# Turning the first batch's sums between the second batch's products, with other engines for the copies and another order of mixing

## The chip, the cores and the metric

The kernel runs on one core of a Trainium2 chip. Its engines have a queue of instructions each and work at the same time: TensorE (PE in the profile, its weight loads PEld), VectorE (DVE), ScalarE (ACT), GpSimd (POOL) and SyncE (SP), which issues the DMAs. An engine takes its instructions in order; an instruction that waits holds up all behind it on that engine. The metric is the time on the device in microseconds (us), as a median of several runs.

## The reference

Attention with a local window and block summaries, and behind it a mixing layer with low rank and a layer of 2048 hidden values, in fp32. There are 4 batches, 8 heads, 768 tokens, 64 values a head, so a row of 512 values for each token.

```python
scores_l = scale * q @ k^T          # kept where |i - j| < 16
scores_s = scale * q @ max over blocks of 32 of k + log(32)
a = softmax([scores_l, scores_s])
x = a @ [v, means over blocks of 32 of v]     # (batch, 768, 512)
h = x^T @ U @ V                               # mixing over tokens, rank 32
u = x + h^T
out = u + relu(u @ w_ch1) @ w_ch2             # 512 -> 2048 -> 512
```

## The kernel before

The order of all instructions is written by hand: the schedule is manual, so each engine's queue has the order of the program's text. Products in full precision are made of fp32r parts: a value is split into a high part (a copy by ACT) and the rest (a subtraction by DVE or POOL), and three products of parts are added (`split`).

PSUM has 8 banks of 128x512 fp32. Tiles of `bank` get them in the order in which they came free in the program, and a bank is free when the last instruction that reads it is done. Copies, temporary rows and outputs share 8 places in SBUF, the tag `val`, by the same rule.

*The first batch* (`sts[0]`) goes through the hidden layer while its weights arrive, are converted, split and stored for later (the loop over `f`, 16 tiles of 128 hidden values). For each `f` and each half `hf` of the tokens (384), `up` makes the hidden values (12 matmuls into a bank) and `down_rows` adds the product with the second weight to sums (9 matmuls). The sums are `accs[0]` and `accs[1]`: three banks each, 128 tokens by 512 values, held through the whole loop; two banks are left for all else. In between, one step of the second batch's attention and mixing has its place after each product (`place`, 58 steps at places 6 to 63; the last seven are `operand_steps(st, 1)`).

`operand_steps` first adds mixing's product to the rows `st.x`, two tiles of 128 tokens at a time (`mix_rows` with k = 0, 1, 2: two matmuls L730, an addition on DVE L734), then turns tokens to columns (`turn_tokens`, L739, with k = 0, 1 for token tiles 3 to 5 and k = 2, 3 for tiles 0 to 2) and makes and splits the operands of the next batch's products (`operands`).

*The hand-over.* When the first batch's sums are done, each sum is copied out of PSUM (`leave_rows`, L955), turned by three PE transposes per 128 columns (`finish_rows`, L963), added to `u`'s two parts on DVE (L966 reads PSUM and SBUF, L967 reads two SBUF tiles) and sent out by a DMA on SP's queue (L968). A half has four such finishes, c = 0 to 3. In the kernel before, the first half's copies stand before the last nine matmuls L942 of the second half, its four finishes right behind them; then come the second half's copies, and its four finishes stand in the list `behind`.

*The other batches* use a scheme with fewer products for the up layer (`up_phase`): per pair p of hidden tiles seven products of six matmuls (L1203) into banks x and y, with results moved by ACT (L1225, L1237, L1249, L1262) and DVE (L1229, L1242, L1263). `up_phase` yields after each product; the loop at the end of the program counts these steps from i = 0 and puts the next batch's attention and the list `behind` between them. Pair 0 has five steps (its last two products come in pair 1's turn), each later one seven: x, y, third and second of the pair before among them. After four of a pair's products `prepare` splits the next unit of stored weights (ACT L186, POOL L187); when both units of a loaded piece are split, a DMA for the next piece (`whole<-up`, L877) is issued four steps later. These DMAs, the outputs L968 and the next batch's loads (k L208, q L214 and L215, v rows L253) stand in one SP queue. The next batch's steps stand at i = 4, 7, 10, 14, 17, 20 and so on: scores at 4 and 14 (24 small matmuls, L377), exponentials at 4, 7, 14 and 17 (DVE L403, ACT L413), key maxima (L319, L336) at 7, a transpose on DVE (L433) and five loads at 10.

The entries of `behind` are spread by

```python
ends = spread(behind, 2, 2 + 2 * len(behind))   # every second step from i = 2
...
do(steps.get(i, ()))    # the next batch's attention
do(ends.get(i, ()))     # the entries of behind
tick()                  # weight loads that are due
```

Of the kernel before, what the change touches and what calls it, by code (L numbers as in the profile page):

```python
# [32 lines left out]
NC = DM // P  # L33
# [48 lines left out]
def f32(ap):  # L82
    return ap.bitcast(F32)
# [3 lines left out]
def body(ctx: ExitStack, tc, q0, q1, k, v, vn, uv, w1, w2, mask, ident, rep, out):  # L87
    nc = tc.nc
# [10 lines left out]
    def bank(name):  # L99
        return psum.tile([P, 512], F32, name=name, tag="bank")  # L100
# [13 lines left out]
    def op_place(k):  # L114
        return wt.tile([P, 4 * NH], F32, name="place", tag=f"op{k}")
# [18 lines left out]
    for i in range(4):  # L134
        t = op_place(i)
# [57 lines left out]
    def new_batch(b):  # L193
        st = Batch()
        st.b = b
        st.qt, st.kt, st.km, st.vt, st.vn, st.vsum, st.neg = ({} for _ in range(7))
        st.e, st.at, st.psx, st.t4, st.u = ({} for _ in range(5))
        st.op, st.tmp, st.h = ({} for _ in range(3))
        st.ps_s, st.ps_t, st.ps_m, st.ps_r, st.ps_u, st.ps_n = ({} for _ in range(6))
        return st  # L200
# [392 lines left out]
        mix_s_out(st, c, 2)  # L593

    def operand_steps(st, i):
        return [(mix_rows, st, i, k) for k in range(3)] + [(operands, st, i, k) for k in range(4)]

    def one_bank_steps(st):

# [48 lines left out]
        for n, x in enumerate(operand_steps(st, 0)):  # L648
            todo.insert(at + 2 + 2 * n if n < 6 else todo.index((products, H - 1)), x)
        return todo + [(mix, st, 2), (mix_back, st, 2)] + operand_steps(st, 1)  # L650

    def later_steps(st):

        todo = [(later_step, st, i) for i in range(STEPS)]
        for n, x in enumerate(operand_steps(st, 0)):
            todo.insert(MIX[0] + 3 + 2 * n, x)
        return todo + operand_steps(st, 1)
# [278 lines left out]
    def down_rows(acc, f, g, first, last):  # L936

        gh, gl = g
        for t in range(NH // P):
            sl = slice(t * P, (t + 1) * P)  # L940
            for j, (part_w, gt) in enumerate(((0, gh), (0, gl), (1, gh))):
                nc.tensor.matmul(  # L942
                    acc[t],
                    gt[:, sl],
                    w_split[1, f][:, part_w],
                    start=(first and j == 0),
                    stop=(last and j == 2),
                )

    def leave_rows(acc):  # L950

        rows = []
        for t, ps in enumerate(acc):
            r = mo.tile([P, DM], F32, name="r", tag="val", bufs=VALS)
            (nc.vector.tensor_copy if t == 1 else nc.scalar.copy)(r, ps)  # L955
            rows.append(r)
        return rows

    def finish_rows(st, hf, rows, c):

        ps = bank("ps_o")
        for t, r in enumerate(rows):
            nc.tensor.transpose(ps[:, t * P : (t + 1) * P], r[:, c * P : (c + 1) * P], ident_sb)  # L963
        o = mo.tile([P, DM], F32, name="o", tag="val", bufs=VALS)[:, :NH]
        uh, ul = st.u[hf]
        nc.vector.tensor_tensor(o, ps[:, :NH], f32(uh)[:, c], ALU.add)  # L966
        nc.vector.tensor_tensor(o, o, f32(ul)[:, c], ALU.add)  # L967
        nc.sync.dma_start(out=out[c, :, hf * NH : (hf + 1) * NH], in_=o)  # L968


    sts = [new_batch(b) for b in range(B)]
# [3 lines left out]
    st = sts[0]  # L975
# [183 lines left out]
    accs = [None, None]  # L1159
    prev = None  # L1160
    for f in range(NF):
# [27 lines left out]
        run(turn)  # L1189
        turn = begin_turn(f + 3)  # L1190
    rows = leave_rows(accs[0])
    down_rows(accs[1], NF - 1, prev[2], False, True)
    for c in range(NC):
        finish_rows(st, 0, rows, c)
    rows = leave_rows(accs[1])


    def product(ps, a, b, first=False):
# [115 lines left out]

    UP, DOWN = 7 * NF // 2 - 2, NF * NU
    FIRST_STEPS = 15
    behind = [(finish_rows, sts[0], 1, rows, c) for c in range(NC)]
    for b in range(1, B):
        cur, ahead, after = ([*sts, None, None][b + i] for i in range(3))
        todo = later_steps(ahead) if ahead else []  # L1320
# [25 lines left out]
        behind = [(finish, cur, hf, c) for hf in range(2) for c in range(NC)]  # L1346
# [94 lines left out]
```

## Time and profile before

| | |
|---|---|
| median of 3 runs | 666.86 us (666.3 to 669.9) |
| the profiled execution | 668.33 us |
| its span, first to last instruction | 666.50 us |
| granted TensorE clock, mean | 0.997 |
| PE, busy | 640.6 us (96% of the span) |
| DVE, busy | 371.7 us (56%) |
| ACT, busy | 358.5 us (54%) |
| POOL, busy | 361.0 us (54%) |
| DMA | 116.13 MB, mean 174 GB/s |

The span is the profiled execution's from its first instruction to its last; the time has 1.83 us around it. Busy shares are means over the whole span, and stages differ. Rows of the timeline give the start from the span's beginning, the length, the engine, the line, the operation, what is written and read, and in brackets the idle time before and what ended it. A modelled matmul is longer than its distance to the next, since matmuls overlap. The hand-over from the first batch to the second lies at about 223 us.

### The profile page before, as it was taken

To read this page: it belongs to the slowest core of one execution; us is meant where nothing else is said; L and a number is where in the kernel's file an instruction comes from. 1 tells how busy PE (TensorE), PEld (TensorE's weight loads), DVE (VectorE), ACT (ScalarE), POOL (GpSimd) and SP (SyncE) were. 2 spreads that over 40 slices of the span, in tenths; PEclk is the share of its full clock that TensorE was granted. 3 is DMA by queue.
4 is the path that set the end of the run, shared out by engine and by line. 5 is a ranking of instruction groups with operands and counts; after the bars stand their busy time and mean duration, and the time that the engine had idled before them with its cause. 6 is when DMAs were issued, how large, how long until landed. Compare 5 with 4: busy or idle time off the path is not lost.

```text
span 666.5 us, 14015 instructions
## 1 busy us (share of the span) xinstructions
PE 640.6 (96%) x5232; PEld 562.6 (84%) x5232; DVE 371.7 (56%) x1006; ACT 358.5 (54%) x803; POOL 361.0 (54%) x402
## 2 busy tenths in 40 slices
PE   5899999999999898999999999999999999999997
PEld 4789889988888797997787899997787899998885
DVE  5578866668777763567544645566644521232223
ACT  4666666655553555765453467665453365553322
POOL 5424975965577676762336487662334375653310
PEclk9999999999999998999999999999999999999999
DMA  8997497766774268787457059787441055331002
GB/s 219 228 367 239 135 315 240 230 173 195 227 225 163 72 178 265 213 251 203 147 142 205 25 171 325 228 247 204 138 143 59 24 171 178 112 126 64 32 1 94
DMA packets 76420, 116.13 MB, mean 174 GB/s; under 512 B 6976, under 2 KB 52928, under 8 KB 76352
## 3 DMA queue, kind: packets, MB, share of 16 engines
q1 hardware_dynamic: 76352, 115.24, 57.1%
q8 instruction: 41, 0.67, 0.4%
q14 instruction: 27, 0.22, 0.1%
HBM read 91.10 MB, written 24.12 MB: 173 GB/s over the span
## 4 chain that ended last, share of the span: by engine, by line
PE 83%; DVE 4%; DMA 4%; ACT 3%; POOL 2%; issue 2%; SPq 1%; ACTq 0%; POOLq 0%; DVEq 0%
PE acc L1288 30%; PE ps_h L1203 25%; PE acc L942 7%; PE ps_h L920 7%; PE ps_x L494 3%; PE ps_s L354 2%; PE ps_o L739 2%; PE ps_s L377 2%; DMA place<-in_uv 1%; DMA place<-in_q 1%; PE ps_m L666 1%; DMA whole<-up 1%; PE ps_t L463 1%; PE ps_x L480 1%; POOL place L187 1%
## 5 line engine op out<-in xcount | busy, mean ns | idle before, releaser
L187 POOL TENSOR_TENSOR parts<-whole,parts 128x512 fp32r<-128x512 f32 (+1 forms) x144 | 180.5, 1262 | 160.4 <-ACT parts L186 151.3
L1288 PE MATMUL acc<-parts,gh 128*128 128x512 f32 x576 | 192.3, 399 | 0.0
L1203 PE MATMUL ps_h<-op,parts 128*128 128x384 f32 x1008 | 187.5, 340 | 3.2 <-ACT place L1262 2.9
L1203 PEld LDWEIGHTS ps_h<-op,parts 128*128 128x128 f32 x1008 | 175.4, 189 | 6.2 <-ACT place L1262 3.2
L1288 PEld LDWEIGHTS acc<-parts,gh 128*128 128x128 f32 x576 | 108.1, 188 | 23.7 <-issue 1.7
L1288 PE MATMUL acc<-parts,gl 128*128 128x512 f32 x288 | 112.6, 391 | 0.0
L1273 DVE SCALAR_TENSOR_TENSOR gl<-place,gh 128x768 fp32r<-128x768 f32 x48 | 56.2, 1171 | 97.1 <-ACT gh L1272 97.1
L186 ACT CAST parts<-whole 128x512 fp32r<-128x512 f32 (+1 forms) x144 | 83.6, 584 | 9.9 <-DMA whole<-up 8.2
L920 PE MATMUL ps_h<-place 128*128 128x384 f32 x384 | 74.5, 342 | 0.0
L1272 ACT ACTIVATE gh<-place 128x768 fp32r<-128x768 f32 x48 | 40.6, 846 | 60.0 <-PE acc L1288 59.9
L413 ACT ACTIVATE e<-e,neg 128x120 f32<-128x120 f32 x144 | 46.3, 386 | 47.4 <-DVE neg L403 45.7
L942 PE MATMUL acc<-place,gh 128*128 128x512 f32 x192 | 68.4, 410 | 1.3 <-POOL place L187 1.3
L920 PEld LDWEIGHTS ps_h<-place 128*128 128x128 f32 x384 | 65.9, 188 | 1.0 <-DVE place L721 0.3
L162 POOL TENSOR_SCALAR val<-place 128x512 f32<-128x512 f32 (+1 forms) x30 | 47.0, 1582 | 30.8 <-ACT place L149 14.2
L1288 PEld LDWEIGHTS acc<-parts,gl 128*128 128x128 f32 x288 | 54.2, 188 | 9.9 <-DVE gl L1273 0.3
L187 POOL TENSOR_TENSOR place<-val,place 128x512 fp32r<-128x512 f32 x29 | 39.4, 1378 | 18.6 <-ACT place L186 15.3
L187 POOL TENSOR_TENSOR op<-tmp,op 128x384 fp32r<-128x384 f32 x24 | 25.4, 1067 | 39.2 <-ACT op L186 39.2
L942 PEld LDWEIGHTS acc<-place,gh 128*128 128x128 f32 x192 | 35.6, 188 | 10.5 <-POOL place L187 3.2
L403 DVE CUSTOM_DVE_ANT_0 e<-ps_s,mask_sb 128x120 f32<-128x120 f32 x144 | 32.5, 276 | 13.3 <-PE ps_s L377 8.5
L942 PE MATMUL acc<-place,gl 128*128 128x512 f32 x96 | 37.6, 392 | 0.0
L932 ACT ACTIVATE gh<-ps_h 128x384 fp32r<-128x384 f32 x32 | 15.7, 490 | 36.4 <-PE ps_h L920 36.0
L1263 DVE TENSOR_TENSOR place<-place,ps_h 128x384 f32<-128x384 f32 x24 | 13.3, 553 | 38.4 <-ACT place L1262 38.3
(124 smaller groups left out, 858.8 us busy)
## 6 DMA issues: line engine op xcount, KB each, us to landing
place<-in_w SPq DMA_DIRECT2D x32, 512.0 KB, 5.6
whole<-up SPq DMA_DIRECT2D x24, 512.0 KB, 3.9
whole<-down SPq DMA_DIRECT2D x24, 512.0 KB, 3.7
whole<-up SPq DMA_DIRECT2D x24, 384.0 KB, 3.3
vt<-in_v SPq DMA_DIRECT2D x48, 146.2 KB, 4.1
kt<-in_k SPq DMA_DIRECT2D x24, 288.0 KB, 5.4
out_t<-o SPq DMA_DIRECT2D x32, 192.0 KB, 2.2
there<-squares SPq DMA_DIRECT2D x16, 384.0 KB, 4.4
```

The lines of the kernel that those rows point to most:

```text
L162: nc.gpsimd.tensor_scalar(f32(bits), f32(hi), 0.0, None, ALU.mult)
L186: nc.scalar.copy(hi, val)
L187: engine.tensor_tensor(lo, val, f32(hi), ALU.subtract)
L403: nc.vector.tensor_tensor_reduce(out=e[:, u, :], in0=ps[:, i * KC : (i + 1) * KC], in1=mask_sb[:, m, :], scale=-SCALE, scalar=BIG, op0=ALU ...
L413: nc.scalar.activation(e[:, u, :], e[:, u, :], AF.Exp, bias=st.neg[h][:, u : u + 1], scale=-1.0,)
L494: nc.tensor.matmul(ps[32 * i : 32 * i + 32, u * DV : (u + 1) * DV], at[:KC, i, u], vt[u % 2][:, (u // 2) * 2 + (i // 2 + u) % 2], start=Tr ...
L920: nc.tensor.matmul(ps[:, :NH], w_split[0, f][:, c % 2, part_w, c // 2], ut[:, c, :], start=(n == 0), stop=(n == 3 * NC - 1),)
L942: nc.tensor.matmul(acc[t], gt[:, sl], w_split[1, f][:, part_w], start=(first and j == 0), stop=(last and j == 2),)
L1203: nc.tensor.matmul(ps, a[:, sa, i], b[:, sb, i], start=(first and n == 0), stop=(n == 5), skip_group_check=not first,)
L1272: nc.scalar.activation(gh, h, AF.Relu)
L1273: nc.vector.scalar_tensor_tensor(gl, h, 0.0, f32(gh), ALU.max, ALU.subtract)
L1288: nc.tensor.matmul(acc[t], gt[:, sl], w[:, part_w], start=(f == 0 and j == 0), stop=(f == NF - 1 and j == 2),)
```

## The change

Three edits. The first half's four finishes are taken from the place behind the last sums and put at the head of `behind`, ahead of the second half's four; the list has eight entries then, at steps 2, 4, to 16 of the second batch's up products. The second half's sums are copied out right after the first entry. Of the three copies of a half, DVE makes the first and the third and ACT the second, where ACT made two. And `mix_rows` is called for k = 1, 2, 0.

```diff
     def operand_steps(st, i):
-        return [(mix_rows, st, i, k) for k in range(3)] + [(operands, st, i, k) for k in range(4)]
+
+        return [(mix_rows, st, i, k) for k in (1, 2, 0)] + [(operands, st, i, k) for k in range(4)]
...
             r = mo.tile([P, DM], F32, name="r", tag="val", bufs=VALS)
-            (nc.vector.tensor_copy if t == 1 else nc.scalar.copy)(r, ps)
+            (nc.scalar.copy if t == 1 else nc.vector.tensor_copy)(r, ps)
             rows.append(r)
...
     rows = leave_rows(accs[0])
     down_rows(accs[1], NF - 1, prev[2], False, True)
-    for c in range(NC):
-        finish_rows(st, 0, rows, c)
-    rows = leave_rows(accs[1])
+    rows = {0: rows}
...
-    behind = [(finish_rows, sts[0], 1, rows, c) for c in range(NC)]
+
+    def finish_first(hf, c):
+
+        finish_rows(sts[0], hf, rows[hf], c)
+        if (hf, c) == (0, 0):
+            rows[1] = leave_rows(accs[1])
+
+    behind = [(finish_first, hf, c) for hf in range(2) for c in range(NC)]
```

## The prediction

> **What bounds the kernel now.** I read the page first: TensorE (PE) is busy for 96% of the span, so only time in which PE stands still, or runs at a lower clock, can be won. Then the waits of PE; those around the change are
>
> ```profile
> PE 640.6 (96%) x5232; PEld 562.6 (84%) x5232; DVE 371.7 (56%) x1006; ACT 358.5 (54%) x803; POOL 361.0 (54%) x402
> PE ps_h L1203 <- ACT place L1262: 2.9, 1, 2.9
> PE ps_o L963 <- DVE r L955: 1.3, 1, 1.3
> PE ps_o L963 <- ACT r L955: 1.1, 1, 1.1
> PE ps_o L739 <- DVE x L734: 0.8, 1, 0.8
> ```
>
> The middle two are the hand-over from the first batch to the second. PE's rows of the timeline (start, length, what) show them:
>
> ```profile
> 223.03 0.40 PE L942 MATMUL acc<-place,gh 128*128 128x512 f32 x1
> 224.54 1.80 PE L963 MATMUL ps_o<-ident_sb,r 128*128 128x128 f32 x12 [1.11 <-ACT r L955]
> 226.09 3.38 PE L1203 MATMUL ps_h<-op,parts 128*128 128x384 f32 x18
> 229.31 0.27 PE L963 MATMUL ps_o<-ident_sb,r 128*128 128x128 f32 x1
> 230.88 0.44 PE L963 MATMUL ps_o<-ident_sb,r 128*128 128x128 f32 x2 [1.29 <-DVE r L955]
> 236.62 0.49 PE L963 MATMUL ps_o<-ident_sb,r 128*128 128x128 f32 x3
> 236.87 2.33 PE L1203 MATMUL ps_h<-op,parts 128*128 128x384 f32 x12
> 239.04 0.49 PE L963 MATMUL ps_o<-ident_sb,r 128*128 128x128 f32 x3
> 246.50 6.54 PE L1203 MATMUL ps_h<-op,parts 128*128 128x384 f32 x36
> 255.92 6.02 PE L1203 MATMUL ps_h<-op,parts 128*128 128x384 f32 x24 [2.87 <-ACT place L1262]
> ```
>
> After the last sum (223.03) PE waits for copies of the first half's rows, turns them in one block, computes three products, and then waits for the middle copy of the second half's rows, which stands on DVE behind the additions of all four turned blocks. The largest wait is 25 us on, at 255.92. The chain that ended last tells where it comes from:
>
> ```profile
> 214.08 2.09 PE acc L942 x9
> ...
> 233.42 0.78 PE ps_s L377 x24
> ...
> 237.11 2.09 PE ps_h L1203 x12
> ...
> 241.18 1.26 DVE o L967
> 242.46 0.33 SPq L968
> ...
> 245.81 7.05 DMA whole<-up
> ...
> 252.94 0.23 ACT parts L186
> ...
> 255.49 0.38 ACT place L1262
> ```
>
> An output DMA (L968) holds the SP queue until DVE has added (L967); behind it stand five loads and then a weight load (L877), issued at 245.81, landed at 252.86; ACT can't split it before, and ACT's later copy L1262 is what PE waits for. The wait has a tail, in the windows of PE (length, busy, then the granted clock):
>
> ```profile
> 229.74:233.15 3.41, 2.27 (x14) 1.00 0.65 190
> 253.63:257.05 3.42, 1.13 (x6) 1.00 1.08 308
> 257.05:260.46 3.41, 3.41 (x13) 0.50 0.79 245
> 659.82:663.23 3.41, 1.74 (x16) 1.00 0.75 276
> ```
>
> The stretch with PE busy for 1.13 us was followed by 3.41 us at half clock; the hand-over's (2.27 busy) wasn't.
>
> **The change, part by part.** Steps are counted as the loop over the up products does: one product of six matmuls each.
>
> *Turning between products.* One product is 2.09/2 = 1.05 us (the x12 row of the chain). Removed: from the last sum to the turns, 224.54 - 223.03 - 0.23 (a sum's own spacing, the chain's 2.09 for nine) = 1.28; in the block of twelve, 226.09 - 224.54 = 1.55 against 4 x 0.35 = 1.40 for turns of three placed singly, 0.15. The 0.35 is the 0.25 between the rows at 236.62 and 236.87 and, as an estimate, 0.1 for the end of the product before, which overlaps the first of them. Then 230.88 - 229.31 - 0.12 (a third of 0.35) = 1.45 at the second wait. Together 2.9. What covers the new copies: the first two products need neither rows nor copies, only operands, whose last part DVE has finished by 223.0. They last 2.1 us, in which DVE makes its two copies by 224.8.
>
> ```profile
> 222.44 0.56 DVE L187 TENSOR_TENSOR op<-ps_o,op 128x384 fp32r<-128x384 f32 x1 [1.26 <-ACT op L186]
> ```
>
> ```profile
> L955 DVE COPY r<-acc x2: 677/679/681, 223.4 to 230.1; 128x512 f32<-128x512 f32 x2
> L955 ACT COPY r<-acc x4: 578/586/589, 223.9 to 226.3; 128x512 f32<-128x512 f32 x4
> L966 DVE TENSOR_TENSOR o<-ps_o,place x8: 550/552/560, 225.4 to 240.6; 128x384 f32<-128x384 f32 x8
> L967 DVE TENSOR_TENSOR o<-o,place x8: 558/595/1249, 226.0 to 241.2; 128x384 f32<-128x384 f32 x8
> ```
>
> The second half's rows leave after the turn at step 2 (PE about 226.8); DVE's additions and two copies there take 0.55 + 0.56 + 2 x 0.68 = 2.5, done by about 229.5, while PE has two products and the 24 score matmuls until 229.6, and the first bank that must come from those rows is asked for at about 230. Nothing is late by this list; a miss costs its own length. I take 2.9; ends 2.4 (the two wait rows alone) and 3.2 (the count of PE's work below, 252.87 - 249.67).
>
> *The copies' engine.* Two more copies on DVE (2 x 0.68), two fewer on ACT (2 x 0.59). PE no longer stands behind them, so 0 to PE; if the products don't cover, one copy, 0.68, later. A gain of 0.59 at the first hand-over is part of the 1.28 already.
>
> *Mixing's order.* The wait of 0.84 at 213.54 looks like its target:
>
> ```profile
> 212.81 0.67 DVE L734 TENSOR_TENSOR x<-x,ps_u 128x512 f32<-128x512 f32 x1
> 213.54 0.55 PE L739 MATMUL ps_o<-ident_sb,x 128*128 128x128 f32 x3 [0.84 <-DVE x L734]
> ```
>
> The first turn reads token tiles 3 to 5; now the last addition writes 4 and 5, after it 0 and 1. So the data are earlier. But six of eight PSUM banks hold sums then, and two serve all else in turn: the last mixing's bank, then the next up product's, then the turn gets the first of these again, whose release is that same addition. I take 0; the other end is -0.84 (a bank that comes free otherwise). No loss: the later turns that need tiles 0 and 1 stand two places on. In later batches PE has no wait at L739 (its row counts one in all), so 0 there.
>
> *The SP queue, and the wait at 255.92.* Every output DMA moves. Before the loads of step 10 there now stand the first half's four, instead of all eight; the fourth stands at step 8, where the second half's fourth stands now, with the same DVE work around it. PE reaches the turn at step 8 at 223.26 + 9 x 1.05 + 0.78 (scores) + 3 x 0.35 = 234.5, instead of 239.04: 4.5 earlier (0.78 is the chain's L377 row). So 242.46 becomes 238.0, and the five loads follow as now. New: the second half's first output, at step 10, stands between them and the weight load of step 11, 0.43 of SP time (0.33 by its row, and 0.1 to the next issue as an estimate), if DVE has its sum by about 241.0. Before that DVE has two instructions more,
>
> ```profile
> 242.35 0.54 DVE L1229 TENSOR_TENSOR place<-place,ps_h 128x384 f32<-128x384 f32 x1
> 242.82 0.96 DVE L433 STREAM_TRANSPOSE squares<-e 128x768 f32<-128x768 f32 x1
> ```
>
> and the additions of 0.55 and 0.56 to 1.25: from 238.0 that gives 240.6 to 241.3. The weight load goes out at 245.81 - 4.5 + 0.43 = 241.7, and PE resumes at 255.92 - 4.5 + 0.43 = 251.85, 4.1 earlier. Ready would it be at 223.26 + 21 x 1.05 + 2 x 0.78 + 8 x 0.35 = 249.67; so a wait of 2.2 stays where 3.05 is lost now (255.92 - 252.87, the end of the row at 246.50 less the 0.17 by which modelled ends overlap). Of the 4.1, 3.2 is the hand-over on the full count and 0.9 the shorter wait. Ends: 6.2 if the load lands early enough that nothing is waited for (255.92 - 249.67); 2.0 if three long L967 (0.7 each) hold the queue before it.
>
> *The clock.* 24 matmuls took 6.02 after the wait, against 2 x 2.09 = 4.18 at full clock: 1.84, of which 0.1 is the usual start; 1.7. A wait of 2.2 leaves up to 2.0 idle in one stretch of 3.41 (1.4 busy); 1.74 busy kept the clock (659.82), 1.13 didn't, and the stretch boundaries needn't fall so. I take the clock as kept: -1.7; other end 0. [...]
>
> After 256 us the list of PE's waits holds nothing of size, so what is won there is kept; loads and splits follow PE's steps and shift with it.
>
> Sum: 4.1 + 1.7 = 5.8. The profiled execution took 668.33 (span 666.50 and 1.83 around it): 662.5. It stands 1.5 above the median of 666.86; made against the median, 661.1.
>
> **The rivals.** *The half clock stays* (a wait over 2 us falls in one stretch): 666.86 - 4.1 = 662.8. For: 1.4 busy lies between the two rows. Against: the idle time must lie in one stretch.
>
> *The weights land when they do now.* PE arrives 3.2 earlier and waits as much longer: 666.9. The DMA shares speak for and against:
>
> ```profile
> 242.00:244.00 2.00, 1.00 0.30 102
> ...
> 252.00:254.00 2.00, 1.00 1.01 405
> ```
>
> Full engines at the landing, but 0.30 when the loads begin, so the queue runs from their issue and an earlier issue lands earlier. Half of it gives 664.8.
>
> *Slower: outputs before the weight loads.* From step 10 to 16 each second-half output waits for DVE at SP's head, ahead of the loads of steps 11, 14 and 18; now only step 8's does. L967's spread (558 to 1249 ns) is the price: with the long one all eight times, 0.69 x 8 = 5.5 late at step 16, and the load of step 18 directly behind. PE then waits as long for its weights, and the half clock returns: 661.1 + 5.5 + 1.7 = 668.3. It is a loss from a lateness of 4.1 on. Against: DVE (the third busy time) has room to catch up,
>
> ```profile
> 230.88:241.40 10.52, 10.52 (x83) 10.04 (x84) 8.28 (x29) 5.83 (x15) 8.49 (x13) 1.00 0.62 196
> 241.40:252.90 11.50, 11.50 (x86) 10.91 (x84) 6.49 (x24) 4.11 (x10) 6.16 (x8) 1.00 0.75 232
> ```
>
> 2.2 + 5.0 = 7.2 us idle in both, for the first half's additions that move in (4 x 1.15 = 4.6). [...]
>
> *No effect of the row order:* taken as the forecast; with its 0.84 the time is 660.3.
>
> **How the numbers follow.** Forecast (4.1 and the clock) 0.5; half clock stays 0.25; weights land as now or half as late 0.2; slower 0.05. The time is the likeliest one's, 661.1; its own range is 658.9 (5.8 + 2.1, no wait left) to 663.2 (hand-over 2.0 and the clock). For 8 in 10 I go from 659.0 to 664.3, into the third. About 0.5%, 3.3 us, is what a measurement tells from no change: faster than 663.5 are the first two and a little of the third, 0.77; within, 0.19; slower 0.04.
>
> **What would show it.** After: L1203 directly behind L942 with no PE wait on L955; L739 still waiting about 0.8 for L734; the output of step 8 at about 238 on SP and the weight load of step 11 at 241.7; a PE wait on L1262 of about 2 near 252; no row at 0.50. Wrong it is if that wait is 3 or more, if L877 stands behind L968 for microseconds, or if a new PE wait names a bank (L955, L966).

## The result, and the profile after

| | before | after |
|---|---|---|
| median | 667.96 us (666.3 to 669.9) | 662.41 us (661.54 to 663.52) |
| ratio | | 0.9927, 95% interval 0.9899 to 0.9956 |
| profiled execution, span | 668.33, 666.5 us | 663.06, 661.3 us |
| from the start of the last sum's matmul to the span's end | 443.5 us | 437.9 us |

The change makes the kernel faster by 0.7%. Beside the later experiments the same two kernels gave 0.9913 (0.989 to 0.9937) with a median of 660.91 after. The last row is worked out from the L942 row at 223.03 of before and at 223.35 of after (lines are one lower or higher after the change); it leaves out the start of the kernel, which varies by 2 us and more from run to run (the batch's first L942 stands at 57.27 and 57.61 in these two profiles, at 60.64 in one of those below), and it is used for all kernels below: 5.6 us between the two profiles. Two runs of those below took 2210 us (the kernel before) and 899 us (the copies alone), where all others lie between 658 and 672; the ratios and the mean clocks leave them out.

PE's waits after, from the list of waits, those around the change:

```profile
PE ps_h L1202 <- ACT place L1261: 1.8, 1, 1.8
PE ps_o L740 <- DVE x L735: 0.9, 1, 0.9
```

Both waits of the hand-over (1.1 and 1.3) are gone; the largest went from 2.9 to 1.8; the wait at the first turn of tokens is where it was. PE's rows of the timeline:

```profile
223.35 0.39 PE L943 MATMUL acc<-place,gh 128*128 128x512 f32 x1
223.58 3.31 PE L1202 MATMUL ps_h<-op,parts 128*128 128x384 f32 x18
226.73 0.49 PE L964 MATMUL ps_o<-ident_sb,r 128*128 128x128 f32 x3
226.97 2.33 PE L1202 MATMUL ps_h<-op,parts 128*128 128x384 f32 x12
...
234.92 0.49 PE L964 MATMUL ps_o<-ident_sb,r 128*128 128x128 f32 x3
...
245.83 4.42 PE L1202 MATMUL ps_h<-op,parts 128*128 128x384 f32 x24
252.06 4.44 PE L1202 MATMUL ps_h<-op,parts 128*128 128x384 f32 x24 [1.82 <-ACT place L1261]
```

The products follow the last sum without a gap, each turn takes 0.24 to 0.3 to the next product's row, and 24 matmuls after the wait take 4.44 us, not 6.02. The windows of PE around the wait (length, busy, granted clock) show that the clock stayed full: 2 us with almost no work, and 1.00 throughout.

```profile
250.00:252.00 2.00, 0.24 (x2) 1.00 0.97 345
252.00:254.00 2.00, 1.94 (x11) 1.00 1.11 285
254.00:256.00 2.00, 2.00 (x14) 1.00 0.98 308
```

Why this stretch didn't bring the half clock is taken up below, with the experiments on the clock.

SyncE's rows of the timeline show the outputs (L969) in their new places: step 8's, the five loads, step 10's output, and then the weight load (L878).

```profile
238.65 0.33 SPq L969 DMA_DIRECT2D out_t<-o  x1
239.08 0.39 SPq L208 DMA_DIRECT2D kt<-in_k  x1
239.52 0.60 SPq L214 DMA_DIRECT2D qz<-in_q  x1
240.17 0.60 SPq L215 DMA_DIRECT2D qz<-in_q  x1
240.87 1.02 SPq L253 DMA_DIRECT2D stage<-in_vn  x2
241.99 0.38 SPq L969 DMA_DIRECT2D out_t<-o  x1
242.46 0.38 SPq L878 DMA_DIRECT2D whole<-up  x1
```

The chain that ended last runs through the same load as before:

```profile
242.46 6.54 DMA whole<-up
...
249.08 0.23 ACT parts L186
...
251.64 0.38 ACT place L1261
...
252.06 4.44 PE ps_h L1202 x24
```

### The profile page after: what moved, and what is told of

Read it like the earlier page. It is cut to its first block, busy times and chain, and to the rows that moved or that the text cites. A ratio compares the mean times of both kernels' runs of the same rounds, so it can differ in the third digit from the quotient of the medians.

```text
span 661.3 us, 14015 instructions
## 1 busy us (share of the span) xinstructions
PE 638.6 (97%) x5232; PEld 561.1 (85%) x5232; DVE 374.4 (57%) x1008; ACT 357.5 (54%) x801; POOL 361.5 (55%) x402
## 4 chain that ended last, share of the span: by engine, by line
PE 83%; DMA 5%; DVE 4%; ACT 3%; POOL 2%; issue 1%; SPq 1%; ACTq 0%; POOLq 0%; DVEq 0%
PE acc L1287 30%; PE ps_h L1202 24%; PE acc L943 8%; PE ps_h L921 7%; PE ps_x L494 3%; PE ps_s L354 3%; PE ps_o L740 2%; PE ps_s L377 2%; DMA place<-in_q 1%; DMA qz<-in_q 1%; PE ps_m L667 1%; DMA whole<-up 1%; PE ps_t L463 1%; PE ps_x L480 1%; POOL parts L187 1%
```

## The experiments

Ratios are to the kernel before on the same chip; "from the last sum" is the profile's span less the start of the last L942 (or its new line), as in the table above. A single run scatters by 2 us, and a profile is one run, so both columns are to be read together.

| kernel | median | ratio, 95% interval | from the last sum |
|---|---|---|---|
| turns alone | 663.91 | 0.9958, 0.9928 to 0.9988 | 437.7 |
| copies alone | 667.31 | 0.9988, 0.9963 to 1.0012 | 443.5 |
| row order alone | 667.00 | 0.9989, 0.9965 to 1.0014 | 443.5 |
| before, wait filled | 666.38 | 0.9980, 0.9957 to 1.0002 | 441.2 |
| before, weight loads early | 668.35 | 1.0008, 0.9989 to 1.0028 | 442.5 |
| after, weight loads early | 667.08 | 0.9996, 0.9978 to 1.0014 | 442.0 |
| after, first turn ahead | 663.01 | 0.9922, 0.9893 to 0.9950 | 437.2 |
| after, both of these | 665.71 | 0.9967, 0.9948 to 0.9985 | 443.2 |
| after, again | 660.91 | 0.9913, 0.9890 to 0.9937 | 437.4 |
| before, v rows later | 663.49 | 0.9944, 0.9922 to 0.9966 | 438.7 |
| after, v rows later | 661.55 | 0.9914, 0.9895 to 0.9933 | 436.1 |
| after, first turn ahead, v rows later | 659.46 | 0.9886, 0.9864 to 0.9907 | 435.9 |

**The three edits one by one.** The moved finishes alone:

```diff
 # the kernel after, with these two lines as before
-        return [(mix_rows, st, i, k) for k in (1, 2, 0)] + ...
+        return [(mix_rows, st, i, k) for k in range(3)] + ...
-            (nc.scalar.copy if t == 1 else nc.vector.tensor_copy)(r, ps)
+            (nc.vector.tensor_copy if t == 1 else nc.scalar.copy)(r, ps)
```

> The kernel after, with the copies' engines (ACT makes two of three) and mixing's order as before: the moved finishes alone. Theory (the move carries all of it): about as fast as the changed kernel, 662.4, up to 0.3 us slower, because ACT's second copy now stands before the copy that the third product waits for. No PE wait on L955, a wait of about 1.8 on the ACT copy behind the T3 product, no half clock. Rival (the copies' engine carries the hand-over): a PE wait of 0.6 or more returns at the hand-over, 663.5 or more.

From the last sum it takes 437.7 us, as the changed kernel does (437.9, 437.4), and no wait on a copy came back. Its median is higher than the changed kernel's (663.91 against 662.41 and 660.91), and the half clock, of which below, accounts for a part: five of its ten runs have a mean clock of 0.995 or less, of the changed kernel's ten none (mean 0.9966 against 0.9985). Its five runs at 0.998 or more have a mean of 662.6 us, the changed kernel's nine 661.6 (662.5 for the four beside the result, 660.9 for the five later ones). So a gain of about 1 us from the other two edits together isn't excluded, and why the clock of this kernel was lower more often isn't known: its one profile has no half clock before PE's work is done. The opposite, the copies alone (the kernel before, with DVE for t = 0 and 2):

> The kernel before, with DVE making two of three copies. Theory: about the time of before, within 0.5 us: the first half's turns start some 0.4 us earlier, and the second half's wait some 0.65 longer for DVE's second copy behind the additions; the wait near 256 and its half clock stay. Rival (ACT's two copies are what the hand-over costs): 1 us or more faster.

443.5, as before. Its rows show the exchange, a first wait of 0.80 for 1.11 and a second of 1.48 for 1.29:

```profile
223.10 1.82 PE L963 MATMUL ps_o<-ident_sb,r 128*128 128x128 f32 x12 [0.80 <-DVE r L955]
...
229.55 0.83 PE L963 MATMUL ps_o<-ident_sb,r 128*128 128x128 f32 x3 [1.48 <-DVE r L955]
```

And the row order alone (the kernel before, with k in 1, 2, 0):

> The kernel before, with mixing's rows in the order 1, 2, 0. Theory (the turn waits for the bank that the last addition frees): the time of before, and PE still waits 0.8 to 0.9 us for L734 at the first turn of tokens, near 213. Rival (it waits for data): that wait is gone and the time 0.84 us shorter.

443.5 again, and its list of waits keeps the one it might have removed:

```profile
PE ps_o L739 <- DVE x L734: 0.9, 1, 0.9
```

So the data of its own token tiles aren't what the turn waits for. With the turn put ahead of the last addition,

```diff
-        return [(mix_rows, st, i, k) for k in (1, 2, 0)] + [(operands, st, i, k) for k in range(4)]
+        return [(mix_rows, st, i, 1), (mix_rows, st, i, 2), (operands, st, i, 0), (mix_rows, st, i, 0)] + [
+            (operands, st, i, k) for k in range(1, 4)
+        ]
```

> The changed kernel, with the first turn of tokens put ahead of mixing's third row pair, so that neither its data nor its bank come from the last addition. Theory (bank): PE's wait of 0.86 at that turn goes, and the time is 0.8 to 0.9 us shorter, 661.6. Rival (DVE is late there by itself, behind the conversion of weights): the wait moves to the next turn or to the mixing product and the time stays.

the wait is in PE's list no more, and from 200 to 230 us none came in its place. The gain lies ahead of the last sum: from the first L942 of the batch (57.61 in the changed kernel, 60.64 here) to the last (223.35 and 225.38) it is 165.7 and 164.7 us, 1.0 less. All three kernels with the turn ahead have 164.7 to 164.8 there, all others 165.7 to 166.0. The ratio (0.9922 beside 0.9927 and 0.9913) can't tell that apart. That it is the bank, and not another tie between the turn and the addition (both touch the tile x), is argued from the order in which banks come free; no run separates the two.

**The half clock.** The kernel before, with eight matmuls that nothing reads put into the wait:

```diff
             do(ends.get(i, ()))
+            if b == 1 and i == 20:
+                spare = half_bank("spare")
+                for n in range(8):
+                    nc.tensor.matmul(spare, cur.op["B11"][:, 0, 0, :P], cur.op["B11"][:, 0, 0], start=(n == 0), stop=(n == 7))
             tick()
```

> The kernel before, with eight matmuls of no use (1.4 us of PE) put into PE's wait near 254, ahead of the product that waits; nothing reads them. Theory (the half clock follows from PE being idle for most of a 3.4 us stretch): the product starts at the same time, the stretch at half clock is gone, and the time is 1.7 us shorter, near 665. Rival (the half clock has another cause, or the matmuls only push PE back): a half clock as before and the same time, or 1.4 us longer.

```profile
245.96 6.54 PE L1203 MATMUL ps_h<-op,parts 128*128 128x384 f32 x36
252.33 1.55 PE L1336 MATMUL spare<-op 128*128 128x384 f32 x8
254.81 4.44 PE L1203 MATMUL ps_h<-op,parts 128*128 128x384 f32 x24 [0.92 <-ACT place L1262]
```

The matmuls don't push the product back (it starts 8.85 us after the x36 row, before 255.92 - 246.50 = 9.42), and its 24 matmuls take 4.44 instead of 6.02. From the last sum it is 2.3 us shorter, of which 1.6 are the clock and 0.6 the earlier start, which the edit doesn't explain. Its ten runs have a mean clock of 0.9987, the kernel before 0.9969 over 70 runs. The median fell by 1.4, with an interval that just reaches no change.

Where the wait falls may decide too. In the trace of the kernel before, the granted clock goes down at 257.05 and again 409.6 us later, after the last instruction; that is 120 times 3.413 us, the length of the half clock at 257.05. In the changed kernel's trace it goes down once, at 659.90, when PE's work is done. Counted back from these points in steps of 3.413 us (an estimate from these two traces), the wait of before left 1.13 us of work in one stretch (253.63 to 257.05), and half clock followed; the changed kernel's wait of 1.8 left 1.65 (250.30 to 253.71), and the clock stayed full. No other stretch of the two, from 12 us to the last matmul, has less than 1.74. The kernel before with weight loads early has a wait of 2.6 us in its profile, with a mean clock of 1.000. So the length of a wait doesn't settle the clock by itself. The work left in one stretch of 3.413 us agrees with both traces, with the limit between 1.13 and 1.65 us; that it is what decides is the author's reading of two traces.

**What holds the weight load.** First its order: due a step earlier, and ahead of the step's other DMAs.

```diff
-            due.append(4)
+            due.append(4 if key[0] == "down" else 3)
...
+            tick()
             do(steps.get(i, ()))
             do(ends.get(i, ()))
-            tick()
```

> The kernel before, with the weight loads of the up products due one step earlier and put ahead of that step's other DMAs on SP, so that the load behind the five of step 10 goes ahead of them. The hand-over is left as it was. Theory (the wait near 256 is SP's order, and the half clock its tail): wait and half clock are gone, 2.9 + 1.7 = 4.6 us faster, near 662.3 against a median of 666.9, and the two waits at the hand-over stay at 1.1 and 1.3. Rival (the DMA engines' rate sets the landing, not the issue): the load lands as late as before, the wait stays within 1 us, and the time too.

> The changed kernel with the same earlier weight loads. Theory: its remaining wait of 1.8 goes, 660.6. The distance to the kernel before with earlier loads is then the hand-over alone, 2.9 to 3.2 us. Rival (the outputs between the products delay later weight loads as well): a new wait on a weight load of 1 us or more, and no gain over 662.4.

> The changed kernel with both: earlier weight loads, and the first turn ahead of the third row pair. Theory: 1.8 + 0.85 = 2.7 us under the changed kernel, 659.7. Rival: the two gains don't add up, because the weights become late again when PE arrives earlier, 660.6 or more.

All three missed. In the kernel before, the wait near 256 is gone as expected, but another stands 11 us on, at the next attention's products with v (L494), and the chain shows it behind SP's queue. The round trip of the transposed exponentials (L438, then four L446) goes out late there (L438 at 258.38, behind a weight load at 257.95) and lands late, its last part at about 266.9; the chain gives the wait to the weight load issued right behind them, which landed then too.

```profile
261.25 5.68 DMA whole<-up
266.93 0.21 issue
267.14 0.89 PE ps_x L494 x48
```

In the changed kernel the wait near 252 stays, and grows from 1.8 to 2.9, with another owner:

```profile
243.56 6.77 DMA out_t<-o
...
250.42 0.57 DVE o L967
...
254.25 1.97 PE ps_h L1202 x5
```

The last finish needs a place for its output, and the place is an earlier output whose DMA landed 6.77 us after its issue, behind the weight load and the five loads of step 10. DVE waits for it, ACT for DVE's exponentials, PE for ACT. This version left nothing of the gain (0.9996), and with the first turn ahead little (0.9967): there PE waits 1.4 on the ACT copy and 2.8 at L494, and the trace gives the latter to the round trip itself.

So it doesn't help here to send the load ahead of the others; it can be relieved of what stands ahead of it. The v rows (two loads of 256 KB, L253) of steps 10 and 20 are needed only much later:

```diff
-        if i in (2, 5):
-            load_vsum(st, 1, i // 5)
-        if i in (4, 7):
-            slow.append(add_vsum(st, 1, i // 7))
+        if i in (3, 6):
+            load_vsum(st, 1, i // 6)
+        if i in (5, 8):
+            slow.append(add_vsum(st, 1, i // 8))
```

> The kernel before, with the two loads of v rows of steps 10 and 20, and their additions on GpSimd, moved one step of the attention later (four steps of the products). The weight load of step 11 then stands behind three loads, not five, with half a megabyte less ahead of it. Theory (that load's place in SP's order and in the DMA engines' backlog makes the wait near 256): the load lands near 249.5, the wait of 2.87 and its half clock are gone, 3 to 4.6 us faster, and the hand-over's waits of 1.1 and 1.3 stay. Rival (the landing is bound elsewhere, or another place waits in its stead): a wait of 1 us or more stays between 250 and 270, under 1.5 us faster.

```profile
242.18 0.39 SPq L208 DMA_DIRECT2D kt<-in_k  x1
...
243.99 0.55 SPq L877 DMA_DIRECT2D whole<-up  x1
...
245.06 1.19 SPq L253 DMA_DIRECT2D stage<-in_vn  x2
```

```profile
245.79 10.70 PE L1203 MATMUL ps_h<-op,parts 128*128 128x384 f32 x60
```

60 matmuls run through where the wait was. The weight load goes out 1.1 earlier after the last sum (21.7 for 22.8) and lands 4.6 after its issue, not 7.05. The kernel before is 0.56% faster for it (0.34 to 0.78), and from the last sum 4.8 us shorter: 3.05 of wait and 1.6 of half clock. Its two waits of the hand-over are still 1.1 and 1.3. On the changed kernel:

> The changed kernel with the v rows later. Theory: its wait of 1.8 near 252 goes, DVE's wait for the place of an output (0.7 near 247) too, and it is 1 to 1.8 us faster than the changed kernel. Rival (the next weight load, now behind the rows, is late in its place): the wait moves to 255 to 258 and the time stays.

> The changed kernel once more, beside the kernels below and with more runs, since single runs differ by 2 us with the number of stretches at half clock that they happen to have. Theory: 0.992 to 0.994 of before, and at equal granted clock 4 us shorter (3.2 of the hand-over and 0.9 of the wait that follows), the rest being the half clock behind the wait near 256. Rival (the half clock is chance and not tied to that wait): the gain is 4 us alike at every clock, and the mean clock of both kernels is the same.

From the last sum 436.1 against 437.4 and 437.9: 1.3 to 1.8 shorter, the wait of 1.8 being down to 0.2. The medians (661.55 and 660.91) don't show it, and the intervals overlap. The two kernels with v rows later differ in the change alone, and neither has a wait above 0.3 behind the hand-over: 438.7 - 436.1 = 2.6 us by their profiles, 1.9 by their medians, whose intervals overlap.

> The changed kernel with the v rows later and the first turn of tokens ahead of the third row pair: the version that should beat both. Theory: 1.8 + 0.85 = 2.7 us under the changed kernel, 0.988 to 0.990 of before. Rival: the waits don't add up, 0.992 or more.

This one has the lowest median of all: 0.9886 of before (0.9864 to 0.9907), 1.5 us under the changed kernel, where 2.7 were expected; the intervals still overlap. From the last sum on, PE has one wait above 0.2 us:

```profile
PE ps_h L1204 <- POOL parts L187: 0.3, 1, 0.3
```

## Why the prediction was right, point by point

All times from the start of the last sum's matmul.

*The hand-over, 2.9 with ends 2.4 and 3.2.* Right. PE ended step 20's product after 29.84 us before (252.87 - 223.03) and 26.74 after (245.83 + 4.42 - 0.16 - 223.35): 3.1, the full count's 3.2 rather than the rows' 2.9. With hardly a wait behind it (0.2) it is worth 2.6 (the pair with v rows later, one profile each).

*The copies' engine, 0.* Right from the last sum on: 443.5 with it alone, 437.7 without it. The medians leave room for about 1 us, as said above.

*The row order, 0, with 0.84 as the other end.* Right: the wait is 0.9 in its own run and after the change.

*SP's queue, 4.5 earlier at step 8, less 0.43, hence 4.1 at the resumed product.* Right in its sum, by luck: two misses cancel. PE's turn of step 8 came 16.01 after the last sum before and 11.57 after, 4.4 earlier, as forecast. Its output came 4.1 earlier (19.43 and 15.30), since DVE's addition of the turn before took 0.94 us, not 0.63. The weight load went out 3.7 earlier (22.78 and 19.11) instead of 4.1 (the new output ahead of it cost 0.46), but landed in 6.54 instead of 7.05. The product resumed 4.2 earlier (32.89 and 28.71).

*The wait that stays, 2.0 idle.* 1.82, and 1.55 in the second profile.

*The clock, 1.7.* Right in the profile (24 matmuls in 4.44 for 6.02, 1.6), mis-sized as a term of the median. That the clock was kept was a bet: the forecast reckoned with 1.4 us of work in the stretch at worst, between the 1.13 that was followed by half clock and the 1.74 that wasn't, and the stretch came out at 1.65. The forecast took the half clock as part of every run of the kernel before. It isn't: of 70 runs of it beside the experiments, 17 have a mean clock of 0.9985 or more, which leaves no room for a stretch of 3.41 us at half clock (3.41 x 0.5 / 666.5 lowers the mean by 0.0026). Their mean time is 665.9; the 32 runs with about one stretch's loss have 667.9, the 21 with more 668.9. The mean clock is 0.9969 before and 0.9985 after (ten runs), so the change saves some 0.6 of a stretch, about 1.0 us on average. This is an estimate, since the mean clock also counts the stretch at the very end: in the changed kernel's profile that is all of its loss. 4.2 + 1.0 is the 5.2 that lies between the two ratios measured (4.9 and 5.8 us of 668). The runs without a stretch's loss bear out the 4.2: the changed kernel's five at 0.9985 or more have a mean of 662.0, 3.9 less than the 17. That the medians differ by 5.55, close to the forecast's 5.8, is therefore partly luck. The base moved too: the 666.86 of three runs became 667.96 with a fourth.

*The rivals.* The half clock stayed away after the change. The landing does follow the issue and the bytes ahead of it: with half a megabyte less ahead, the load landed in 4.6 us, not 7.05, and the wait is gone altogether. The long additions that the slower case reckoned with came, without their price here: the DVE additions with two SBUF operands took longer.

```profile
L967 DVE TENSOR_TENSOR o<-ps_o,place x8: 514/551/558, 227.3 to 247.0; 128x384 f32<-128x384 f32 x8
L968 DVE TENSOR_TENSOR o<-o,place x8: 557/738/1286, 227.8 to 247.6; 128x384 f32<-128x384 f32 x8
```

The median of L968 (L967 before) went from 595 to 738 ns, while L967 with its PSUM operand stayed at 551 (552 before). Both traces show when, one by one: the ten of L967 before and of L968 after that took 0.60 to 1.29 us began while POOL was at work, the six of 0.56 while it stood still. What the rival left out is the wait that did show in the changed kernel: DVE's for the place of an output still in flight.

```profile
247.04 0.56 DVE L967 TENSOR_TENSOR o<-ps_o,place 128x384 f32<-128x384 f32 x1 [0.70 <-DMA out_t<-o]
```

Here it cost nothing, since ACT waited for the weight load longer; with that load early it was 3.0 and took the gain. Once the v rows are later, the 0.2 that PE still waits comes along DVE's turns and additions, not from the load.

## What to carry to other kernels

Work that stands in one block between two stages, with its copies and additions on another engine, cost PE its waits here (1.1 and 1.3 us) rather than its matmuls; put between products of the next stage it cost its matmuls alone (0.24 to 0.3 us a turn), since those products didn't need it. What such a move wins ahead of a wait on a DMA is kept only if the DMA goes out earlier too (here 3.7 us): follow the issuing queue through the move, instruction by instruction. To shorten a wait on a load, take other bytes from ahead of it (here half a megabyte, and the wait of 2.9 was gone); sending it earlier than its neighbours moved the wait to them in all three kernels where it was tried.

## What the runs showed of the hardware

A PE wait of 2.9 us was followed by 3.41 us at half clock in the trace of the kernel before (257.05 to 260.46 at 0.50), and by the mean clocks in some runs of the same kernel and not in others (17 of 70 have a mean of 0.9985 or more); it explains much of the scatter: over the 70 runs of the kernel before, a loss of 0.0026 in mean clock goes with 1.6 us. PE didn't have to stand still for all of the 3.41 us ahead of it, as 1.13 us of work there didn't keep the clock; 1.65 us in the changed kernel's trace did. 1.4 us of matmuls with no use (8 of the 12 that take 2.09), put into the wait, brought the work from 252.30 to 255.70 to 2.48 us, and the clock stayed at 1.00.

An output of 192 KB landed 1.9 us after its issue when little was ahead of it (issued at 238.65 in the changed kernel's trace), and 6.77 us after it behind a weight load and the next batch's loads (the changed kernel with weight loads early). Where a buffer is given back by a DMA, that is the time to plan for here.
